# A decode step bound by its K and V stream: w1 loaded second, the MLP moved into the first group, weights in contiguous rows

## The chip, the cores and the metric

The kernel runs on one core of a Trainium2 chip; the other cores are idle. A core has five engines with a queue of instructions each: TensorE (PE in the profile, its weight loads PEld), VectorE (DVE), ScalarE (ACT), GpSimd (POOL) and SyncE (SP). They run independently and wait for each other on semaphores. SP and ACT also issue DMAs, which 16 DMA engines carry out; each engine works through the packets of a queue in the order of their issue. The metric is the device time of one execution, in microseconds (us).

## The reference

The layer is the gated sum of an attention over a cache and of an MLP, for a batch of 8 sequences with one new token each. D is 576, there are 32 heads of 128, 4096 cached positions, and the MLP is 4608 wide. All arrays are bf16.

```python
x = A_x                                             # (8, 1, 576)
g = sigmoid((x * gate_w).sum(-1, keepdims=True))
q = (x @ wq) -> (8, 32 heads, 1, 128)               # wq: 576 x 4096
s = q . k_cache * 128 ** -0.5                       # k_cache: 8 x 32 x 4096 x 128
a = (softmax(s) . v_cache) -> (8, 1, 4096) @ wo     # wo: 4096 x 576
y = layernorm(x)
b = gelu(y @ w1 + b1) @ w2 + b2                     # w1: 576 x 4608, w2: 4608 x 576
return g * a + (1 - g) * b
```

The two caches are 268 MB each, the four weights together about 20 MB. Every byte is read once.

## The kernel before

**Groups.** The 256 pairs of a sequence and a head are worked off in NG = 32 groups of HB = 8 heads of one sequence. A group needs 8 MB of K and 8 MB of V. The 128 partitions hold 8 heads times 16 stretches of 256 positions, so each partition reads one contiguous run of the cache. K comes in two halves of 4 MB, each into a buffer of its own (`KB`, two of them), V in one load of 8 MB into the single buffer `VB`. A fourth large buffer, `RB`, holds one weight after the other: wq, w1, w2, wo.

**Scores.** VectorE multiplies K by the broadcast query in 8 chunks of 32 positions per partition (`mult`, line 448) into the tile `p1`. TensorE sums the products with an identity as its weights: one weight load and 8 matmuls to a chunk (`p_sum`, lines 459 and 461; the helper `held` puts seven of them on line 179). VectorE adds up the last 16 columns (`reduce`, 466). A product chunk has to wait until the sums two chunks earlier have read its half of `p1`.

**Softmax, PV, gathering.** VectorE and ScalarE make the softmax (483 to 499). TensorE multiplies the probabilities by V in 64 matmuls with a weight load each (`pv`, 509); ScalarE evicts (521); TensorE gathers the heads' rows (527), VectorE normalizes one group later (`norm`, 532).

**Order on the engines.** There is no scheduler. Each call of `op` appends an instruction to one engine's list, and each engine runs its list in that order, waiting where an operand is not ready. `aside` does the same with a second semaphore. The function `between(c)` is called between chunks and slips other work into the lists at that place. SP's list holds nearly all loads, so that a load whose buffer is not free holds back all loads behind it. A K half waits for the last product of the half before in its buffer (`k_done`), a V load for the PV of the group before (`v_done`).

**The weights' schedule.** SP issues x, then wq, K and V of group 0. x is transposed on TensorE (`transposed`, 368) so that the contraction runs over partitions: partition p of slice kt stands for row 128 kt + p of the weight. The Q projection takes 40 matmuls (405). Its end frees `RB` for w1 (411). q is broadcast to the partitions by `q_of(b)` for each of the 8 sequences, two matmuls (426) and an eviction (430); the first runs ahead of group 0, the others between its chunks. The up projection (`up_proj`, 547), 216 pairs of a weight load and a matmul of 8 columns, is spread over groups 1 and 2 (`UP`, `NUP`). Behind it w2 takes `RB`. The GELU (`act_h`, 551) and the down projection (`down_proj`, 144 matmuls on line 571) lie in group 3 (`DN`), and wo follows.

**Loops.** The instructions of TensorE are written out for groups 0 to 3, and groups 4 to 29 are turns of a loop (`LOOP`, `emit_loop`). VectorE's loop covers groups 1 to 29. `emit_loop` turns each wait that grows by the same step from turn to turn into a wait on a computed value. The last two groups are written out, and their V comes in smaller parts.

Of the kernel before, what the change touches and what calls it, by code (L numbers as in the profile page):

```python
# [12 lines left out]
B = 8  # L13
# [28 lines left out]
class Stream:  # L42
# [98 lines left out]
def bass_gated_mix__mha_block_cached__mixer_channel_mlp__decode_kernel(  # L141
# [45 lines left out]
    RB = sb("RB", [128, 9 * F // 2], BF16)  # L187
    wq_sb = view(RB, 0, [128, 4, SK])
    wq_t = view(RB, 4 * SK, [128, SK // 2])
    w1_sb = view(RB, 0, [128, 4, F])  # L190
    w1_t = view(RB, 4 * F, [128, F // 2])
    w2_sb = view(RB, 0, [128, NJ, D])
    wo_sb = view(RB, 0, [128, H, D])
    p1 = sb("p1", [128, 2, CT, DH], BF16)
# [66 lines left out]
    def load(engine, dst, src, name, waits=()):  # L261
        return op(engine, lambda e: e.dma_start(dst, src), waits, dma=(nc.alloc_semaphore(name), 16))  # L262
# [7 lines left out]

    c_b2 = op("gpsimd", lambda e: e.memset(b2_4[:], 0.0))
    c_g4 = op("gpsimd", lambda e: e.memset(g4[:], 0.0))
    ld_x = load("sync", x_sb, x_flat, "ld_x")
    ld_gw = load("scalar", gw8, bcast(gate_w), "ld_gw")
    ld_b1 = load("scalar", b1_sb[:, :], B_b1.rearrange("(p j) -> p j", j=NJ), "ld_b1")
    def halves(w):

        return w[512:576, :].rearrange("r (s n) -> (r s) n", s=2)

    ld_wq = [load("sync", wq_sb, A_wq[0:512, :].rearrange("(kt p) n -> p kt n", p=128), "ld_wqa"),  # L280
             load("sync", wq_t, halves(A_wq), "ld_wqb")]


    def kv_src(cache, n):
# [12 lines left out]
    def load_v(n):  # L297
        nV[0] += 1
        src = kv_src(A_v_cache, n)
        t = op("sync", lambda e: e.dma_start(VB[:, :, :], src), [v_done.get(n - 1)], dma=(sV, 16 * nV[0]))  # L300
        v_land[n] = [(t, VB, 0, 0, NTT)]

    def load_v_part(n, buf, at, t0, t1, waits):
# [8 lines left out]

    load_k(0)
    load_k(1)
    load_v(0)


    def memset(engine, ap, value):
        return op(engine, lambda e: e.memset(ap, value))
# [48 lines left out]
    def transposed(src, srcz, col, waits):  # L368
        last = None
        for kt in range(NKF + 2):  # L370
            o = up_ps[:, col + kt * B:col + (kt + 1) * B]
            i = src[:, kt * 128:(kt + 1) * 128] if kt < NKF else srcz[:, kt - NKF, :, :].rearrange("b r s -> b (r s)")
            last = aside("tensor", lambda e, o=o, i=i: e.matmul(o, lhsT=i, rhs=ident[0:B, 0:B], start=True, stop=True),
                      waits if kt == 0 else ())
        return last
# [22 lines left out]
    for half in range(2):  # L398
        for h in range(4):
            for kt in range(NKT):  # L400
# [7 lines left out]
        a_Q.append(aside("scalar", lambda e, half=half: e.activation(  # L408
            out=Q4[:, half * 512:(half + 1) * 512], in_=tr_ps[half][:, :], func=ACT.Copy, scale=inv_sqrt_dh), [p_Q]))

    ld_w1 = [load("sync", w1_sb, B_w1[0:512, :].rearrange("(kt p) f -> p kt f", p=128), "ld_w1a", [p_Q]),
             load("sync", w1_t, halves(B_w1), "ld_w1b")]


    last = NG - 1
    UP, NUP = 1, 2
    DN = UP + NUP
    AP = 30
    LOOP = {"tensor": DN + 1, "vector": 1}
    SLOT = {"tensor": 16, "vector": 128}  # L420

    a_qb, v_mult, v_red, p_sum, v_nm, a_exp, v_P, p_pv, a_ev, p_oz, v_norm, v_rs, p_z, v_rz = ({} for _ in range(14))
# [1 line left out]
    def q_of(b):  # L424
        for i in range(2):
            t = aside("tensor", lambda e, i=i: e.matmul(
                qb_ps[64 * i:64 * i + 64, :], lhsT=Sel[:, b, :],
                rhs=bass.AP(tensor=Q4, offset=i * DH, ap=[[pstride(Q4), 128], [2 * DH, NHG], [1, DH]]),
                start=True, stop=True), [*a_Q, c_Sel, a_qb.get(b - 1)] if i == 0 else ())
        a_qb[b] = aside("scalar", lambda e: e.activation(out=q_bc[:, b, :], in_=qb_ps[:, :], func=ACT.Copy), [t])  # L430
# [109 lines left out]
    def up_proj(j0, j1):  # L540
        for jt in range(j0, j1):
            for kt in range(NKF + 2):
                o, n, at = up_ps[:, jt * B:(jt + 1) * B], 128, kt * F + jt
                if kt >= NKF:
                    o, n, at = up_ps[64 * (kt - NKF):64 * (kt - NKF) + 64, jt * B:(jt + 1) * B], 64, NKF * F + jt
                w = bass.AP(tensor=RB, offset=at, ap=[[pstride(RB), 128], [NJ, n]])
                st["p_up"] = aside("tensor", lambda e, w=w, o=o, kt=kt: e.matmul(  # L547
                    o, lhsT=w, rhs=yT_sb[:, kt, :], start=(kt == 0), stop=(kt >= NKF)),
                    [*ld_w1, v_yT] if jt == kt == 0 else ())
# [13 lines left out]
            out=hT_sb[:].rearrange("p f b -> p (f b)"), in0=hb, in1=t2, op=ALU.mult), [t])  # L563

    def load_w2():
        st["ld_w2"] = load("sync", w2_sb, B_w2.rearrange("(p j) n -> p j n", j=NJ), "ld_w2", [st["p_up"]])

    def quarters(lhsT, w, first, stop, waits):

# [52 lines left out]


    done_a = [0]
    q_of(0)
    q_group(0)
    for n in range(NG):
        for e, l0 in LOOP.items():
            if l0 <= n <= AP:
                S.marks.setdefault(e, []).append(len(S.ops[e]))  # L630

        def between(c, n=n):
            if c == 1 and 1 <= n < last:
                norm(n - 1)
            if n == last and c == NCK:
                load_v_part(n, KB[0], 0, 0, NTK, [k_done[NKH * n]])
                t0 = NTK
                for nt in V_LAST:
                    load_v_part(n, VB, t0 - NTK, t0, t0 + nt, [p_pv[n - 1]])
                    t0 += nt  # L640
            if UP <= n < UP + NUP:
                i = (n - UP) * NC + c
                up_proj(i * NJ // (NUP * NC), (i + 1) * NJ // (NUP * NC))
            if n == DN and c == 1:
                act_h()
            if n == DN and c >= NC - 3:
                down_proj((c - NC + 3) * NJ // 3, (c - NC + 4) * NJ // 3)
            if n >= AP and c % NCK == 2 and done_a[0] < NHG - 1:
                a_proj(done_a[0])
                done_a[0] += 1  # L650
            if n == 0 and c + 1 < B:
                q_of(c + 1)

        scores(n, between)
        if n < last:
            q_group(n + 1)
        softmax(n)
        if n < last:
            total(n)
        if n < last - 1:  # L660
            load_k(NKH * (n + 1))
            load_k(NKH * (n + 1) + 1)
            pv(n, (0,))
            evict(n)
            gather(n)
            if n == UP + NUP - 1:
                load_w2()
            if n + 1 < last - 1:
                load_v(n + 1)
        if n == last - 2:  # L670
            load_v_part(last - 1, VB, 0, 0, NTK, [v_done[n]])
        if n == last - 1:
            load_k(NKH * last)
            load_k(NKH * last + 1)
            load_v_part(n, VB, NTK, NTK, NTT, [v_done[n - 1]])
            pv(n, (0,))
        if n == DN:
            b_out()
            load_wo()
        if n == last - 4:  # L680
            load_b2()
            b_gate()
# [64 lines left out]
```

## Time and profile before

| | |
|---|---|
| median of 3 runs | 1302.79 us (1302.63 to 1303.39) |
| profiled execution | 1302.9 us, of which the span from first to last instruction is 1301.0 |
| mean granted clock of TensorE | 0.844 |
| busy: TensorE matmul, VectorE, ScalarE, GpSimd | 812.0, 849.9, 71.1, 9.6 us |
| DMA | 557.18 MB, mean 428 GB/s |
| K half, from issue to landing (median of 64) | 26.6 us |
| V load, from issue to landing (median of 30) | 31.6 us |

A line such as `24.78 4.49 DVE L448 TENSOR_TENSOR ... x2` reads: start, length, engine and line, operation, tiles written and read, how many instructions were merged. An engine's name with a q behind it is its sequencer, which waits or issues. In windows of time the columns are the window, its length, the busy time of TensorE, its weight loads, VectorE, ScalarE and GpSimd with the instructions in brackets, the granted clock of TensorE, the DMA engines' share of busy time and GB/s. A DMA queue's line gives packets, MB and the packets' time as a share of 16 engines; q1 is SP's, q10 ACT's, q8 fetches instructions.

### The profile page before, as it was taken

The numbers are of one execution on the slowest core, as the hardware profiler recorded it, in microseconds if no ns is written. First come the engines' busy times: TensorE is split into PE (matmuls) and PEld (weight loads), VectorE is DVE, ScalarE is ACT, GpSimd is POOL, SyncE is SP. The second block draws the span as 40 slices with busy tenths as digits, with TensorE's granted clock in tenths as the row PEclk, the third lists the DMA queues.
The fourth block names the chain that finished last, engine by engine and source line by source line (L and its number), as shares of the span: only waits on it lengthen the run. The fifth ranks groups of instructions, "written<-read, shape, count | busy, mean of one in ns | idle before, by whom it ended". The sixth has DMA issues, their size and how long they took to land.

```text
span 1301.0 us, 10743 instructions
## 1 busy us (share of the span) xinstructions
PE 812.0 (62%) x5020; PEld 169.5 (13%) x3228; DVE 849.9 (65%) x1073; ACT 71.1 (5%) x160; POOL 9.6 (1%) x19
## 2 busy tenths in 40 slices
PE   3658746366656565756665765666666666576566
PEld 0113201100111110111110111110011110011112
DVE  3657566277666668666668766667766667766684
ACT  3100000000000000000000000000000000000000
POOL 0000010000000000000000000000000000000000
PEclk8868887688887898888889888789878888978898
DMA  9999999999999999999999999999999999999997
GB/s 398 420 454 422 427 428 443 410 433 432 435 437 429 428 433 432 441 429 433 426 433 434 433 439 427 428 434 434 433 434 433 433 427 433 431 440 429 428 432 321
DMA packets 20894, 557.18 MB, mean 428 GB/s; under 512 B 2048, under 2 KB 6160, under 8 KB 7056
## 3 DMA queue, kind: packets, MB, share of 16 engines
q1 hardware_dynamic: 20624, 556.95, 99.6%
q8 instruction: 10, 0.16, 0.1%
q10 hardware_dynamic: 256, 0.03, 0.0%
q14 instruction: 4, 0.03, 0.0%
HBM read 556.96 MB, written 0.01 MB: 428 GB/s over the span
## 4 chain that ended last, share of the span: by engine, by line
DMA 69%; DVE 18%; PE 9%; issue 3%; SPq 0%; DVEq 0%; ACT 0%
DMA KB<-in_A_k_cache_dram 67%; DVE p L448 16%; PE psb L179 7%; DVE s_sb L466 2%; DMA VB<-in_A_v_cache_dram 2%; PE psb L459 1%; SPq L262 0%; DVEq L134 0%; PE psb L509 0%; DVE P L495 0%; PE psb L571 0%; PE psb L547 0%; PE psb L516 0%; ACT E L492 0%; DVE mA L483 0%
## 5 line engine op out<-in xcount | busy, mean ns | idle before, releaser
L448 DVE TENSOR_TENSOR p<-KB,q_n 128x4096 bf16<-128x4096 bf16 x256 | 582.0, 2284 | 318.1 <-DMA KB<-in_A_k_cache_dram 309.0
L179 PE MATMUL psb<-p,ident 128*128 128x512 bf16 x1792 | 484.4, 416 | 0.0
L459 PE MATMUL psb<-p,ident 128*128 128x512 bf16 x256 | 110.2, 431 | 283.2 <-DVE p L448 283.0
L466 DVE TENSOR_REDUCE s_sb<-psb 128x32 f32<-128x512 f32 x256 | 175.1, 684 | 84.7 <-PE psb L179 84.7
L509 PE MATMUL psb<-VB,P 128*32 128x512 bf16 x1984 | 178.8, 539 | 8.5 <-DMA VB<-in_A_v_cache_dram 8.5
L459 PEld LDWEIGHTS psb<-p,ident 128*128 128x128 bf16 x256 | 26.1, 102 | 699.1 <-DVE p L448 620.0
L516 PE MATMUL psb<-rs,ones 128*128 128x8 f32 x64 | 18.7, 365 | 151.3 <-DVE rs L499 151.3
L509 PEld LDWEIGHTS psb<-VB,P 128*32 128x32 bf16 x1984 | 65.2, 131 | 108.9 <-issue 86.5
L495 DVE TENSOR_SCALAR P<-E,own 128x256 bf16<-128x256 bf16 x248 | 51.6, 283 | 17.9 <-ACT E L492 17.9
L527 PE MATMUL psb<-selO,O_sb 128*128 128x8 f32 x256 | 34.4, 261 | 22.6 <-ACT O_sb L521 22.6
L516 PEld LDWEIGHTS psb<-rs,ones 128*128 128x128 f32 x64 | 15.7, 304 | 203.1 <-DVE rs L499 202.2
L436 ACT ACTIVATE q_n<-q_bc 128x128 bf16<-128x128 bf16 x32 | 9.9, 309 | 529.8 <-DVE p L448 529.7
L527 PEld LDWEIGHTS psb<-selO,O_sb 128*128 128x128 f32 x256 | 31.5, 194 | 37.9 <-ACT O_sb L521 37.9
L521 ACT ACTIVATE O_sb<-psb 128x512 f32<-128x512 f32 x32 | 19.1, 596 | 276.1 <-PE psb L509 276.1
L492 ACT ACTIVATE E<-s_sb,mD 128x256 bf16<-128x256 f32 x32 | 16.2, 507 | 145.4 <-DVE mD L491 145.4
L547 PEld LDWEIGHTS psb<-yT_sb,RB 128*128 128x128 bf16 (+1 forms) x216 | 19.8, 165 | 28.3 <-issue 26.3
L441 ACT ACTIVATE OT_sb<-O_n 128x8 bf16<-128x8 bf16 x31 | 7.4, 237 | 233.2 <-DVE O_n L533 233.2
L547 PE MATMUL psb<-yT_sb,RB 128*128 128x8 bf16 (+1 forms) x216 | 19.9, 226 | 0.0
L483 DVE TENSOR_REDUCE mA<-s_sb 128x1 f32<-128x256 f32 x32 | 13.4, 420 | 1.1
L498 DVE TENSOR_REDUCE es<-E 128x1 f32<-128x256 bf16 x32 | 13.1, 411 | 0.0
L499 DVE TENSOR_SCALAR rs<-own,es 128x8 f32<-128x8 f32 x32 | 7.5, 234 | 1.1
L592 POOL TENSOR_TENSOR Q<-Q,b 104x144 f32<-104x144 f32 x1 | 0.6, 589 | 1009.6 <-DMA b<-in_B_b_dram 1009.6
(76 smaller groups left out, 106.4 us busy)
## 6 DMA issues: line engine op xcount, KB each, us to landing
KB<-in_A_k_cache_dram SPq DMA_DIRECT2D x64, 4096.0 KB, 26.6
VB<-in_A_v_cache_dram SPq DMA_DIRECT2D x2, 4096.0 KB, 24.8
RB<-in_B_w_dram SPq DMA_DIRECT2D x1, 5184.0 KB, 34.8
RB<-in_B_w_dram SPq DMA_DIRECT2D x1, 4608.0 KB, 45.9
RB<-in_A_wo_dram SPq DMA_DIRECT2D x1, 4608.0 KB, 44.5
RB<-in_A_wq_dram SPq DMA_DIRECT2D x1, 4096.0 KB, 12.6
KB<-in_A_v_cache_dram SPq DMA_DIRECT2D x1, 4096.0 KB, 18.9
VB<-in_A_v_cache_dram SPq DMA_DIRECT2D x2, 1024.0 KB, 22.0
```

Source lines behind the costliest of these rows:

```text
L179: return e.add_instruction(mybir.InstMatmult(name=nc.get_next_instruction_name(), engine=mybir.EngineType.PE, ins=[e.lower_ap(rhs), e.lowe ...
L448: v_mult[n, c] = op("vector", lambda e: e.tensor_tensor(out=p1[:, par, :, :], in0=KB[u % NKH][:, t0:t0 + CT, :], in1=qb, op=ALU.mult), [k_ ...
L459: fn = lambda e, r=r: e.matmul(tr_ps[par][:, :], lhsT=ident[:, :], rhs=r, start=True, stop=False)
L466: v_red[n, c] = op("vector", lambda e: e.tensor_reduce(out=s_sb[:, c * CT:(c + 1) * CT], in_=tr_ps[par][:, :].rearrange("p (t c) -> p t c" ...
L483: t = op("vector", lambda e: e.tensor_reduce(out=mA[:, 0:1], in_=s_sb[:, :], axis=AX.X, op=ALU.max), [v_red[n, NC - 1], c_mA])
L492: a_exp[n] = op("scalar", lambda e: e.activation(out=E[:, :], in_=s_sb[:, :], func=ACT.Exp, bias=mD[:, 0:1], scale=1.0), [v_nm[n], v_P.get ...
L495: v_P[n] = op("vector", lambda e, h=h: e.tensor_scalar(out=(P if n < NG - 1 else P_last)[:, :, h, :], in0=E[:, :].rearrange("p (q t) -> p ...
L509: p_pv[n] = op("tensor", lambda e, o=o, tq=tq, at=at, buf=buf: e.matmul(o, lhsT=(P if n < last else P_last)[:, tq, :, :].rearrange("p h t ...
L516: p_z[n] = op("tensor", lambda e: e.matmul(oz_ps[:, HB:2 * HB], lhsT=ones[:, :], rhs=rs[:, :], start=True, stop=True), [v_rs[n], v_norm.ge ...
L521: a_ev[n] = op("scalar", lambda e: e.activation(out=O_sb[:].rearrange("p t d -> p (t d)"), in_=o_ps[n // last][:, :], func=ACT.Copy), [p_p ...
L527: p_oz[n] = op("tensor", lambda e, tt=tt: e.matmul(o, lhsT=O_sb[:, tt, :], rhs=selO[:, tt, :], start=(tt == 0 and n < last), stop=(tt == T ...
L547: st["p_up"] = aside("tensor", lambda e, w=w, o=o, kt=kt: e.matmul(o, lhsT=w, rhs=yT_sb[:, kt, :], start=(kt == 0), stop=(kt >= NKF)), [*l ...
```

## The change

- The layout of wq and w1 in SBUF: partition p now holds rows 4p to 4p + 3 of the first 512 rows, one contiguous run of 32 or 36 KB, where before it held rows p, 128 + p, 256 + p and 384 + p in runs of 8 or 9 KB. x and y are transposed to match: slice kt takes every fourth column.
- w1 goes into `VB`, and SP loads it right behind wq, with no wait. The load of x moves from SP to ACT, ahead of gate_w and b1.
- SP's order at the start becomes wq, w1, K of group 0, then w2 into `RB` (waiting for the Q projection), then V of group 0 (waiting for the up projection, which reads w1 out of `VB`).
- All eight `q_of` and the whole up projection stand ahead of group 0 on TensorE, followed by `act_h`.
- The down projection lies in group 0, a quarter after each of the chunks 3 to 6; wo is loaded after group 0, ahead of V of group 1.
- TensorE's loop begins at group 1.

```diff
-    w1_sb = view(RB, 0, [128, 4, F])
-    w1_t = view(RB, 4 * F, [128, F // 2])
+    w1_sb = view(VB, 0, [128, 4, F])
+    w1_t = view(VB, 4 * F, [128, F // 2])
...
-    ld_x = load("sync", x_sb, x_flat, "ld_x")
+    ld_x = load("scalar", x_sb, x_flat, "ld_x")
...
-    ld_wq = [load("sync", wq_sb, A_wq[0:512, :].rearrange("(kt p) n -> p kt n", p=128), "ld_wqa"),
+    ld_wq = [load("sync", wq_sb, A_wq[0:512, :].rearrange("(p kt) n -> p kt n", kt=4), "ld_wqa"),
              load("sync", wq_t, halves(A_wq), "ld_wqb")]
+    ld_w1 = [load("sync", w1_sb, B_w1[0:512, :].rearrange("(p kt) f -> p kt f", kt=4), "ld_w1a"),
+             load("sync", w1_t, halves(B_w1), "ld_w1b")]
...
-        t = op("sync", lambda e: e.dma_start(VB[:, :, :], src), [v_done.get(n - 1)], dma=(sV, 16 * nV[0]))
+        t = op("sync", lambda e: e.dma_start(VB[:, :, :], src), [v_done.get(n - 1) if n else st["p_up"]], dma=(sV, 16 * nV[0]))
...
     load_k(0)
     load_k(1)
-    load_v(0)
...
-            i = src[:, kt * 128:(kt + 1) * 128] if kt < NKF else srcz[...]
+            i = src[:, kt:NKF * 128:NKF] if kt < NKF else srcz[...]
...
-    ld_w1 = [load("sync", w1_sb, B_w1[0:512, :].rearrange("(kt p) f -> p kt f", p=128), "ld_w1a", [p_Q]),
-             load("sync", w1_t, halves(B_w1), "ld_w1b")]
...
-    UP, NUP = 1, 2
-    DN = UP + NUP
-    LOOP = {"tensor": DN + 1, "vector": 1}
+    LOOP = {"tensor": 1, "vector": 1}
...
-                w = bass.AP(tensor=RB, offset=at, ap=[[pstride(RB), 128], [NJ, n]])
+                w = bass.AP(tensor=VB, offset=at, ap=[[pstride(VB), 128], [NJ, n]])
...
-        st["ld_w2"] = load("sync", w2_sb, B_w2.rearrange("(p j) n -> p j n", j=NJ), "ld_w2", [st["p_up"]])
+        st["ld_w2"] = load("sync", w2_sb, B_w2.rearrange("(p j) n -> p j n", j=NJ), "ld_w2", [p_Q])
...
-    q_of(0)
-    q_group(0)
+    for b in range(B):
+        q_of(b)
+        if b == 0:
+            q_group(0)
+        up_proj(b * NJ // B, (b + 1) * NJ // B)
+    act_h()
+    load_w2()
+    load_v(0)
...
-            if UP <= n < UP + NUP:
-                i = (n - UP) * NC + c
-                up_proj(i * NJ // (NUP * NC), (i + 1) * NJ // (NUP * NC))
-            if n == DN and c == 1:
-                act_h()
-            if n == DN and c >= NC - 3:
-                down_proj((c - NC + 3) * NJ // 3, (c - NC + 4) * NJ // 3)
+            if n == 0 and 3 <= c <= 6:
+                down_proj((c - 3) * NJ // 4, (c - 2) * NJ // 4)
...
-            if n == 0 and c + 1 < B:
-                q_of(c + 1)
...
-            if n == UP + NUP - 1:
-                load_w2()
+            if n == 0:
+                b_out()
+                load_wo()
...
-        if n == DN:
-            b_out()
-            load_wo()
```

More of the change, by code (lines that the diff above doesn't have):

```diff
@@ L371, in transposed @@
             o = up_ps[:, col + kt * B:col + (kt + 1) * B]
-            i = src[:, kt * 128:(kt + 1) * 128] if kt < NKF else srcz[:, kt - NKF, :, :].rearrange("b r s -> b (r s)")
+            i = src[:, kt:NKF * 128:NKF] if kt < NKF else srcz[:, kt - NKF, :, :].rearrange("b r s -> b (r s)")
             last = aside("tensor", lambda e, o=o, i=i: e.matmul(o, lhsT=i, rhs=ident[0:B, 0:B], start=True, stop=True),
```

## The prediction

> **What bounds the kernel now.** I read the page first: engine shares, slices, traffic, chain.
>
> ```profile
> span 1301.0 us, 10743 instructions
> ...
> PE 812.0 (62%) x5020; PEld 169.5 (13%) x3228; DVE 849.9 (65%) x1073; ACT 71.1 (5%) x160; POOL 9.6 (1%) x19
> ...
> DMA  9999999999999999999999999999999999999997
> GB/s 398 420 454 422 427 428 443 410 433 432 435 437 429 428 433 432 441 429 433 426 433 434 433 439 427 428 434 434 433 434 433 433 427 433 431 440 429 428 432 321
> DMA packets 20894, 557.18 MB, mean 428 GB/s; under 512 B 2048, under 2 KB 6160, under 8 KB 7056
> ...
> DMA 69%; DVE 18%; PE 9%; issue 3%; SPq 0%; DVEq 0%; ACT 0%
> ```
>
> No engine is busy over 65%, while the DMA line is full from the first slice to the last but one. The chain names VectorE for 18%, but those steps only wait for the next transfer. Then the busy time by stage, to see whether any stage has a hole that a better order could fill. Columns: window, its length, busy time of five engines, clock, DMA share, GB/s.
>
> ```profile
> 67.00:100.00 33.00, 19.86 (x120) 7.20 (x78) 19.05 (x15) 0.24 (x1) 0.00 (x0) 0.67 1.04 448
> 100.00:133.00 33.00, 28.55 (x232) 13.42 (x183) 23.89 (x32) 1.65 (x4) 0.00 (x0) 0.90 0.97 420
> 133.00:166.00 33.00, 24.35 (x170) 8.22 (x126) 19.36 (x29) 3.65 (x7) 4.48 (x4) 0.79 1.01 435
> 166.00:199.00 33.00, 15.38 (x212) 4.11 (x179) 17.66 (x26) 2.10 (x3) 2.25 (x1) 0.82 0.98 423
> 265.00:1265.00 1000.00, 630.49 (x3614) 112.88 (x2157) 687.26 (x858) 42.09 (x102) 1.24 (x2) 0.85 1.00 432
> ```
>
> A share swings a little above and below 1.00 because whole packets are booked to a window. There is no hole: the groups 1 to 3, where the up and down projections lie now, have the share of the 1000 us behind them. So the time is the first packet's start, plus 557 MB at the engines' rate, plus a tail behind the last packet. The change moves the same 557 MB. It can win only at the start and in the rate of wq, w1 and instruction packets; it can lose by opening a hole.
>
> **The start.** What SP issues, and the first 12 us:
>
> ```profile
> 0.74 0.38 SPq L262 DMA_DIRECT2D p<-in_A_x_dram  x1
> 1.18 0.96 SPq L262 DMA_DIRECT2D RB<-in_A_wq_dram  x2
> 2.18 1.10 SPq L295 DMA_DIRECT2D KB<-in_A_k_cache_dram  x2
> ...
> 20.57 0.93 SPq L262 DMA_DIRECT2D RB<-in_B_w_dram  x2
> ...
> 0.00:2.00 2.00, 0.00 (x0) 0.00 (x0) 0.31 (x2) 0.24 (x1) 1.23 (x10) 1.00 0.03 9
> 2.00:4.00 2.00, 0.00 (x0) 0.00 (x0) 1.86 (x7) 1.99 (x3) 0.36 (x3) 1.00 0.89 230
> 4.00:6.00 2.00, 0.00 (x0) 0.00 (x0) 0.97 (x5) 1.98 (x4) 0.00 (x0) 1.00 1.00 409
> 6.00:8.00 2.00, 0.00 (x0) 0.00 (x0) 0.00 (x0) 1.97 (x3) 0.00 (x0) 1.00 1.03 435
> 8.00:10.00 2.00, 0.30 (x6) 0.24 (x6) 0.74 (x4) 0.70 (x5) 0.00 (x0) 1.00 0.99 418
> 10.00:12.00 2.00, 0.32 (x6) 0.24 (x6) 0.21 (x1) 1.09 (x6) 0.00 (x0) 1.00 1.03 430
> ```
>
> *x goes to ACT's queue.* wq is then SP's first issue, at 0.74 instead of 1.18: 0.44 us sooner for the whole stream. It gains at least 0.3 (x's small packets still share the engines), at most 0.5. I take 0.4. On ACT, x stands ahead of gate_w and b1, which go out about 0.4 us later; gate_w feeds ACT's sigmoid, ahead of x's transposition, and those results are wanted only when wq has landed, 3.6 us after they are ready (the wait of L405 below). b1 is wanted at about 51. Both cost nothing; without that cover, 0.4.
>
> *wq in contiguous rows.* Its 8 KB rows become one 32 KB run per partition, which is what a K load has. From 4 to 12 us wq ran at (409 + 435 + 418 + 430)/4 = 423 GB/s against 432: 4.19 MB take 9.91 against 9.71 us, 0.2 us. The 2 to 4 window carries 0.46 MB where 0.86 would fit, 0.9 us lost, of which 0.2 is the idle share. If long runs mend the remaining 0.7, the gain is 0.9. Bounds 0 and 0.9, taken 0.4: the steady rows show 0.2 for certain, the ramp may be latency as well as short rows.
>
> *w1 in contiguous rows.* Rows of 9 KB become 36 KB. The nearest rows are wq's: at the same 2%, 4.72 MB gain 0.2 us; bounds 0 and 0.4. Taken 0.2. The stationary operands of x and y are now read with a step of 4, in 12 transpositions of 0.05 us each: nothing, behind the same 3.6 us of cover.
>
> **TensorE's loop.** Groups 1 to 3 leave the written-out code. Instruction packets, by two windows (40 to 210 us, then 205 to 1220):
>
> ```profile
> q1 hardware_dynamic: 2429, 72.91, 99.8%
> q8 instruction: 7, 0.11, 0.3%
> ```
>
> ```profile
> q1 hardware_dynamic: 15264, 438.64, 100.3%
> q10 hardware_dynamic: 64, 0.01, 0.0%
> ```
>
> Seven packets of 16 KB came in while TensorE ran written-out code, none while it looped. A packet held one engine 0.3% x 16 x 170 us / 7 = 1.2 us. By the code a group is some 220 weight loads and matmuls: 8 chunks of 9, 64 pairs for PV, about 20 for the sums and the gathering. Four groups, with 432 for the up projection, 288 for the down projection and some 90 before, make 1690, or 240 to a packet. Three groups less save 2.7 packets: spread evenly, 0.2 us; all on the engine that ends last, 3.2; on other engines than the last, 0. I take 0.2, since three packets of seven need not meet on one of 16 engines.
>
> The Trainium skill, Runtime: NRT & Kernel Launch, Instruction fetch mechanics, speaks against this part: a taken branch out of the two-page window forces a fetch, so written-out code is to be preferred. By it 29 loop-backs instead of 26 would fetch again what is saved, and the sum would be 1.0 rather than 1.2 us. The second window, 26 turns without one q8 packet, disagrees, and the measurement decides.
>
> **The moved work: does it open a hole?** After the change the queue holds wq, w1, K of group 0 (two halves), w2, V of group 0, K of group 1, wo, V of group 1. At 432 GB/s: wq 10.9 us, w1 12.3, a K half 9.7, w2 12.3, V 19.4. From 1.8 (2.2, where the 0.89 share puts the first full packet, less 0.4), with 0.3 for the ramp: wq ends at 13.0, w1 25.3, K 44.7, w2 57.0, V 76.4, K of group 1 at 86.1 and 95.8. Each load must be issued about 1.0 us (1.18 to 2.2) before its turn. The price of TensorE's work, with two windows for its granted clock:
>
> ```profile
> 15.16 5.38 PE L405 MATMUL psb<-RB,p 128*8 128x512 bf16 x40 [3.64 <-DMA RB<-in_A_wq_dram]
> ...
> 27.13 0.61 PE L459 MATMUL psb<-p,ident 128*128 128x512 bf16 x1 [5.49 <-DVE p L448]
> 30.57 0.41 PE L426 MATMUL psb<-Q,Sel 128*64 128x512 bf16 x2
> ...
> 36.39 11.53 SPq L295 DMA_DIRECT2D KB<-in_A_k_cache_dram  x2
> 54.23 0.23 DVE L499 TENSOR_SCALAR rs<-own,es 128x8 f32<-128x8 f32 x1
> 55.33 6.49 PE L509 MATMUL psb<-VB,P 128*32 128x512 bf16 x64 [0.22 <-DMA VB<-in_A_v_cache_dram]
> ...
> 82.00:84.00 2.00, 2.00 (x11) 0.62 (x6) 0.71 (x4) 0.24 (x1) 0.00 (x0) 0.50 0.99 426
> 83.53 1.04 PEld L547 LDWEIGHTS psb<-yT_sb,RB 128*128 128x128 bf16 x11 [0.26 <-issue]
> 92.00:94.00 2.00, 2.00 (x14) 0.55 (x6) 2.00 (x2) 0.00 (x0) 0.00 (x0) 1.00 1.18 500
> 93.36 1.78 PEld L547 LDWEIGHTS psb<-yT_sb,RB 128*128 128x128 bf16 x18 [1.43 <-issue]
> 160.30 0.39 ACT L554 ACTIVATE Q<-psb 128x288 f32<-128x288 f32 x1
> 166.06 2.25 POOL L562 TENSOR_TENSOR hT_sb<-Q 128x288 bf16<-128x288 f32 x1 [0.55 <-ACT Q L561]
> ...
> 177.15 0.93 PE L571 MATMUL psb<-RB,hT_sb 128*8 128x144 bf16 x48 [1.94 <-DMA RB<-in_B_w_dram]
> ```
>
> - *w2 waits for the Q projection.* wq lands at about 14.3 (15.16 less 0.4 and 0.4), the projection ends 5.4 later, 19.7; w2's turn is at 44.7. Nothing behind it on SP is due before.
> - *V of group 0 waits for the up projection.* w1 lands 12.0 after wq, about 26.3. 216 pairs of weight load and matmul at 1.78/18 = 0.099 us are 21.4, seven q broadcasts at 0.41 are 2.9: end at 50.6. V must be issued by 56.0. Spare 5.4 us, the smallest of all; with no cover it costs one for one.
> - *K of group 1 waits for group 0's products.* Group 0's sums now start at 50.6 instead of 27.1, 23.5 later. Its K buffers come free at 36.4 + 23.5 = 59.9 and (SP's second issue of that row) 47.6 + 23.5 = 71.1, due at 75.4 and 85.1.
> - *The down projection in group 0.* h is ready 8.0 us (160.30 to 168.31) after the up projection, 58.6; w2 lands at 58. Its first quarter stands behind the fourth chunk, 60 to 62, and so does not wait. Four times 36 matmuls at 0.93/48 are 2.8 us beside VectorE, in place of the q broadcasts. wo can go out at about 71; its turn is 95.8.
> - *V of group 1 waits for PV of group 0.* The softmax ends at 54.5 + 23.5 = 78.0, V lands at 77.4, PV takes 6.5: 84.5. With some 12 for wo it is due at 107. That issue may be held on SP while wo's short rows drain, as a K issue is now: the row below holds two issues from 218.28 to 241.77, with wo in flight, and the window that has it shows no hole beyond wo's slower rows. Costs 0.
>
> ```profile
> 218.28 23.49 SPq L295 DMA_DIRECT2D KB<-in_A_k_cache_dram  x2
> 232.00:265.00 33.00, 12.79 (x90) 3.87 (x76) 10.28 (x22) 1.34 (x3) 0.00 (x0) 0.64 1.04 420
> ```
>
> From group 1 on everything stands as now against the DMA stream, so its shift reaches the last output unchanged.
>
> **Sum.** 0.4 + 0.4 + 0.2 + 0.2 = 1.2 us sooner. The profiled execution took 1302.9 (span 1301.0 and 1.9 around it), 0.1 over the median 1302.79. So 1301.6 by the median; bounds of this case 0.5 and 2.2 us, 1300.6 to 1302.3.
>
> **Rivals.**
> - *Slower: the up projection ends late and V of group 0 opens a hole.* It decides from 5.4 us on: to lose 0.2% it must end 1.2 + 2.6 + 5.4 = 9.2 us late. If the 216 pairs cost twice as much in one run (0.2 us), the end moves by 21.4 to 72 and the hole is 16 us: 1318. For it: 460 instructions in a row, more than the trace ever shows at this pace, and the clock falling after the idle wait for w1. Against it: PV issues 128 in 6.5 us, and the 11 loads at 83.53, at a granted clock of 0.50, cost 0.095 us each, the 18 at 93.36, at a clock of 1.00, 0.099. The Trainium skill, TensorE: Matmul & The Clock Gate, Part 1: after an idle window of about 3.4 us the array runs at half rate until it has been busy as long. By that rule a pair would double while cold; these rows show no such effect on these small matmuls. Chance 0.11, typically 1306 or more.
> - *Faster by over 0.2%.* The ramp mends fully (0.9) and two saved instruction packets were on the engine that ends last (2.4 instead of 0.2): 0.4 + 0.9 + 0.4 + 2.4 = 4.1, about 1299. For it: every such packet delays one engine for good in a stream without holes. Against: nothing shows them on one engine. Chance 0.13.
> - *The layouts do nothing.* The rate of wq and w1 stays, the first packet starts where it did because of x's packets: 1302.6. The 6 to 8 window, 435 GB/s with 8 KB rows, speaks for it. Chance 0.14.
>
> **How the numbers follow.** The likeliest case has 0.62, own range 1300.6 to 1302.3. A measurement of this kernel can tell about 0.2%, 2.6 us, from no change: within it lie the likeliest case and the idle layouts, 0.76; faster 0.13; slower 0.11. The range, 1299.8 to 1303.3, leaves out most of the slow case and half of the fast one.
>
> **What would show it.** wq's first issue at about 0.74 and the 2 to 4 window well above 230 GB/s; the Q projection's first matmul at 14.3 rather than 15.16; the last L547 at about 50 and SP's first V issue right behind it, with DMA shares near 1.00 from 50 to 110; five or fewer q8 packets before the loop; a span of about 1299.8 instead of 1301.0. A DMA share under 0.9 between 56 and 60 would prove me wrong, and so would TensorE waits called issue inside the up projection.

## The result and the profile after

| | before | after |
|---|---|---|
| median | 1302.80 us (22 runs, 1302.55 to 1303.93) | 1300.97 us (22 runs, 1300.67 to 1302.29) |
| ratio | | 0.9986, 95% interval 0.9979 to 0.9992 |
| span of the profiled execution | 1301.0 us | 1299.1 us |
| DMA packets | 20894 | 20124 |
| instruction packets (q8) ahead of the loop | 7 | 5 |

The change gains 1.83 us, 0.14%, and the interval of the ratio leaves out 1. That is 0.6 us more than the 1.2 forecast, and less than the 0.2% (2.6 us) up to which the prediction counted a time as no change. The page of the changed kernel has the same form as before: no engine above 65%, and a DMA line that is full up to the last slice.

```profile
span 1299.1 us, 10783 instructions
...
PE 813.6 (63%) x5020; PEld 166.9 (13%) x3228; DVE 849.8 (65%) x1073; ACT 68.7 (5%) x158; POOL 6.1 (0%) x19
...
DMA  9999999999999999999999999999999999999997
GB/s 405 434 418 422 447 426 438 418 435 435 438 438 428 425 435 434 442 428 430 430 433 433 438 430 440 421 434 429 440 438 426 435 424 435 436 434 438 419 434 335
DMA packets 20124, 557.14 MB, mean 429 GB/s; under 512 B 2048, under 2 KB 6160, under 8 KB 7056
```

What SP issues up to group 1, in the changed kernel (start, length, queue, line, what is written and read):

```profile
0.74 0.88 SPq L262 DMA_DIRECT2D RB<-in_A_wq_dram  x2
1.67 1.18 SPq L262 DMA_DIRECT2D VB<-in_B_w_dram  x2
...
20.09 0.33 SPq L262 DMA_DIRECT2D RB<-in_B_w_dram  x1
50.12 0.33 SPq L302 DMA_DIRECT2D VB<-in_A_v_cache_dram  x1
59.76 11.53 SPq L297 DMA_DIRECT2D KB<-in_A_k_cache_dram  x2
71.33 0.43 SPq L262 DMA_DIRECT2D RB<-in_A_wo_dram  x1
85.68 19.51 SPq L302 DMA_DIRECT2D VB<-in_A_v_cache_dram  x1
```

The moved work on TensorE and the end of group 0's softmax on VectorE. (Line numbers have shifted: 542 is the up projection, 566 the down projection, 494 the softmax's end, 504 PV, 605 the last V parts.)

```profile
14.81 5.25 PE L405 MATMUL psb<-RB,p 128*8 128x512 bf16 x40 [2.43 <-DMA RB<-in_A_wq_dram]
...
27.12 2.22 PE L542 MATMUL psb<-yT_sb,VB 128*128 128x8 bf16 x24 [5.97 <-issue]
...
47.86 2.23 PE L542 MATMUL psb<-yT_sb,VB 128*128 128x8 bf16 x24
61.62 0.74 PE L566 MATMUL psb<-RB,hT_sb 128*8 128x144 bf16 x36
...
79.66 5.97 PE L504 MATMUL psb<-VB,P 128*32 128x512 bf16 x64 [1.18 <-DMA VB<-in_A_v_cache_dram]
```

```profile
77.60 0.23 DVE L494 TENSOR_SCALAR rs<-own,es 128x8 f32<-128x8 f32 x1
```

Windows of the changed kernel; the last two columns are the DMA share and GB/s, and the one before them the granted clock:

```profile
0.00:2.00 2.00, 0.00 (x0) 0.00 (x0) 0.31 (x2) 0.00 (x0) 1.23 (x10) 1.00 0.71 184
2.00:4.00 2.00, 0.00 (x0) 0.00 (x0) 1.72 (x6) 1.91 (x3) 0.36 (x3) 1.00 0.88 328
4.00:6.00 2.00, 0.00 (x0) 0.00 (x0) 0.45 (x4) 1.98 (x4) 0.00 (x0) 1.00 0.65 279
...
56.00:60.00 4.00, 2.11 (x9) 0.19 (x2) 4.00 (x4) 0.00 (x0) 0.00 (x0) 1.00 1.04 449
...
100.00:133.00 33.00, 12.68 (x67) 1.94 (x35) 16.89 (x26) 0.82 (x2) 0.00 (x0) 0.78 1.05 432
265.00:1265.00 1000.00, 630.27 (x3612) 112.23 (x2156) 685.82 (x857) 42.09 (x102) 1.15 (x2) 0.85 1.00 432
```

From 56 to 60, where a late V of group 0 would show, the share is 1.04: no hole. The steady stretch runs at 432 GB/s, as before. So the gain lies at the two ends of the stream, and the end is where most of it is. Four 1-us windows of the last stretch, the six microseconds from 1290 in one window, and the matmuls that wait for the last part of V. First the kernel before:

```profile
1290.00:1296.00 6.00, 4.60 (x82) 3.42 (x82) 0.21 (x1) 0.60 (x1) 0.00 (x0) 0.78 0.63 246
...
1293.00:1294.00 1.00, 1.00 (x14) 1.00 (x11) 0.00 (x0) 0.00 (x0) 0.00 (x0) 0.68 0.62 242
1294.00:1295.00 1.00, 1.00 (x19) 0.94 (x19) 0.00 (x0) 0.00 (x0) 0.00 (x0) 0.50 0.15 57
1295.00:1296.00 1.00, 0.84 (x26) 0.73 (x24) 0.00 (x0) 0.00 (x0) 0.00 (x0) 0.50 0.09 35
```

```profile
1296.41 0.38 PE L610 MATMUL psb<-p,VB 128*128 128x8 bf16 x8 [0.26 <-DMA VB<-in_A_v_cache_dram]
```

Then the changed kernel:

```profile
1290.00:1296.00 6.00, 5.05 (x120) 3.96 (x112) 0.35 (x2) 0.60 (x1) 0.00 (x0) 0.73 0.48 186
...
1292.00:1293.00 1.00, 1.00 (x22) 0.96 (x21) 0.00 (x0) 0.00 (x0) 0.00 (x0) 0.87 0.69 266
1293.00:1294.00 1.00, 0.81 (x24) 0.68 (x23) 0.00 (x0) 0.00 (x0) 0.00 (x0) 0.50 0.21 80
1294.00:1295.00 1.00, 0.58 (x16) 0.41 (x13) 0.12 (x1) 0.00 (x0) 0.00 (x0) 0.50 0.00 0
```

```profile
1294.46 0.38 PE L605 MATMUL psb<-p,VB 128*128 128x8 bf16 x8 [0.26 <-DMA VB<-in_A_v_cache_dram]
```

One engine of 16 that works for a whole microsecond makes a share of 0.06. Before, after most engines had ended by 1294, two or three worked on in the next microsecond (0.15) and one or two in the one after it (0.09). After, the share falls from 0.69 to nothing in two microseconds. The last matmuls start 1.95 us sooner (1296.41 to 1294.46), but the time that an average engine still worked behind 1290 fell by only 0.90 us (6 x 0.63 = 3.78 to 6 x 0.48 = 2.88). The other 1.05 is no shorter stream: it is that the engines end together.

### The profile page after: what moved, and what is told of

Read it like the earlier page. It is cut to its first block, busy times and chain, and to the rows that moved or that the text cites. A ratio compares the mean times of both kernels' runs of the same rounds, so it can differ in the third digit from the quotient of the medians.

```text
span 1299.1 us, 10783 instructions
## 1 busy us (share of the span) xinstructions
PE 813.6 (63%) x5020; PEld 166.9 (13%) x3228; DVE 849.8 (65%) x1073; ACT 68.7 (5%) x158; POOL 6.1 (0%) x19
## 2 busy tenths in 40 slices
DMA packets 20124, 557.14 MB, mean 429 GB/s; under 512 B 2048, under 2 KB 6160, under 8 KB 7056
## 4 chain that ended last, share of the span: by engine, by line
DMA 67%; DVE 18%; PE 11%; issue 3%; SPq 0%; DVEq 0%; ACT 0%
DMA KB<-in_A_k_cache_dram 63%; DVE p L443 15%; PE psb L179 7%; DVE s_sb L461 2%; DMA VB<-in_B_w_dram 2%; DMA VB<-in_A_v_cache_dram 2%; PE psb L542 2%; PE psb L454 1%; DVEq L134 0%; SPq L262 0%; PE psb L504 0%; PE psb L421 0%; SPq L302 0%; DVE P L490 0%; PE psb L566 0%
## 5 line engine op out<-in xcount | busy, mean ns | idle before, releaser
L542 PE MATMUL psb<-yT_sb,VB 128*128 128x8 bf16 (+1 forms) x216 | 20.1, 230 | 6.0 <-issue 6.0
L542 PEld LDWEIGHTS psb<-yT_sb,VB 128*128 128x128 bf16 (+1 forms) x216 | 18.4, 166 | 10.4 <-issue 9.3
```

## The experiments

Two theories were set against each other. A, the prediction's: the end follows the mean load of the 16 DMA engines, so a packet of instructions costs a sixteenth of its 1.1 us. B: the engine that lags most sets the end, so such a packet costs nothing or about 1.1 us. "Before" is between 1302.81 and 1302.90 in the comparisons below. The times of one kernel scatter by about 1 us or more, mostly outside the span from first to last instruction; the spans scatter by 0.3 to 1.0 us. So a difference of 0.2 or 0.3 us between medians is hardly clear of the scatter.

**The parts, undone one at a time.** In the changed kernel, x goes back to SP's queue:

```diff
-    ld_x = load("scalar", x_sb, x_flat, "ld_x")
+    ld_x = load("sync", x_sb, x_flat, "ld_x")
```

> The changed kernel with x loaded on SP again, ahead of wq. Theory A (the transfers' total sets the time, and each part counts with its own share): wq is issued 0.4 us later, so 0.4 us slower than the changed kernel, about 1301.4. Theory B (the one DMA engine that lags most sets the end): the same 0.4, changed by up to 0.5 either way if x's eight packets fall on other engines. Rival, the start is bound by the first packets' latency and not by the issue: 1301.0.

Measured 1301.15 us (ratio 0.9988, 0.9979 to 0.9997): 0.18 more than the changed kernel, within the spread of either. Then wq and w1 in their old rows, with the transposition to match:

```diff
-    ld_wq = [load("sync", wq_sb, A_wq[0:512, :].rearrange("(p kt) n -> p kt n", kt=4), "ld_wqa"),
+    ld_wq = [load("sync", wq_sb, A_wq[0:512, :].rearrange("(kt p) n -> p kt n", p=128), "ld_wqa"),
...
-    ld_w1 = [load("sync", w1_sb, B_w1[0:512, :].rearrange("(p kt) f -> p kt f", kt=4), "ld_w1a"),
+    ld_w1 = [load("sync", w1_sb, B_w1[0:512, :].rearrange("(kt p) f -> p kt f", p=128), "ld_w1a"),
...
-            i = src[:, kt:NKF * 128:NKF] if kt < NKF else srcz[:, kt - NKF, :, :].rearrange("b r s -> b (r s)")
+            i = src[:, kt * 128:(kt + 1) * 128] if kt < NKF else srcz[:, kt - NKF, :, :].rearrange("b r s -> b (r s)")
```

> The changed kernel with wq and w1 in the old layout, rows of 8 and 9 KB, and x and y transposed to match. Theory A: w1's packets held the 16 engines 11.29 us in the old layout against 10.93 in the new one, wq's steady rows differ by 0.2: 0.55 us slower than the changed kernel, about 1301.5. If the ramp of the first packets were mended by long rows, 1.2 slower. Rival, the layouts do nothing: 1301.0. The first matmul of the Q projection should start 0.1 to 0.3 us later than 14.81.

Measured 1301.28 us (0.9988, 0.9979 to 0.9997): 0.31 more, hardly clear of the scatter either. Then TensorE's loop over groups 4 to 29, as before the change:

```diff
-    LOOP = {"tensor": 1, "vector": 1}
+    LOOP = {"tensor": 4, "vector": 1}
```

> The changed kernel with TensorE's groups 1 to 3 written out again, the loop from group 4. Two or three more instruction packets of 16 KB. Theory A: each counts a sixteenth of its 1.1 us, 0.2 us slower, about 1301.2. Theory B: each delays one engine by 1.1 us for good, and the end moves with the engine that lags most: anywhere from 0 to 1.5 us slower, as they fall.

Measured 1302.35 us (0.9995, 0.9986 to 1.0004): 1.38 more. The part to which the prediction gave 0.2 of 1.2 us carries most of the gain.

**The parts, done alone.** The kernel before, with x on ACT's queue and with the rows of wq and w1 and the transposition of the change, and nothing else:

```diff
-    ld_x = load("sync", x_sb, x_flat, "ld_x")
+    ld_x = load("scalar", x_sb, x_flat, "ld_x")
...
-    ld_wq = [load("sync", wq_sb, A_wq[0:512, :].rearrange("(kt p) n -> p kt n", p=128), "ld_wqa"),
+    ld_wq = [load("sync", wq_sb, A_wq[0:512, :].rearrange("(p kt) n -> p kt n", kt=4), "ld_wqa"),
...
```

> The kernel before with x on ACT and wq and w1 in contiguous rows alone; order, buffers and loop as before. Theory A: 0.4 + 0.55 us faster than before, about 1301.85. Theory B: the same for the mean of the engines, while the slowest one may keep its lag or lose it: 1301.2 to 1302.5. If the new order itself brings something, this falls short of the changed kernel by more than the 0.2 of the instruction packets.

Measured 1301.90 us (0.9993, 0.9984 to 1.0002): 0.9 to 1.0 sooner than before. Compared with the changed kernel with its loop at group 4 (1302.35), which differs from it in the order alone, the new order brings nothing (it is 0.45 slower). The order and the loop without x and rows, which is the changed kernel with the first two edits of this section together:

```diff
-    ld_x = load("scalar", x_sb, x_flat, "ld_x")
+    ld_x = load("sync", x_sb, x_flat, "ld_x")
...
-    ld_wq = [load("sync", wq_sb, A_wq[0:512, :].rearrange("(p kt) n -> p kt n", kt=4), "ld_wqa"),
+    ld_wq = [load("sync", wq_sb, A_wq[0:512, :].rearrange("(kt p) n -> p kt n", p=128), "ld_wqa"),
...
```

> The changed kernel with x back on SP's queue and wq and w1 back in rows of 8 and 9 KB: what is left of the change is the order of the loads and TensorE's loop over groups 1 to 29. Undone one by one, x cost 0.18 and the rows 0.31 us. If these add up, 1301.5 beside 1302.8 for the kernel before: the loop and the order then carry 1.3 of the 1.8 us. The prediction's sum gives 0.2 to them, so 1302.6. Theory B allows 1301.0 to 1302.4, by where the instruction packets fall.

Measured 1301.40 us (0.9989, 0.9980 to 0.9998), as expected from adding (1301.5), and not the 1302.6 of the prediction's sum.

**Is it one lagging engine?** An extra load on ACT's queue at the start, into a free stretch of `p1`, with the first products waiting for it. On 17 partitions it should run on one engine. (The Trainium skill, DMA: Bandwidth & Descriptors, section Why a DMA increments its semaphore by 16 and not by 1, under How many engines (k): the largest count up to 16 that divides the partitions, here 1.) The control puts the same bytes on 16 partitions, with `p1[64:80, 1, 0:17, :]` and t=17.

```diff
+    ld_more = load("scalar", p1[64:81, 1, 0:16, :], A_k_cache[0, 0, 0:272, :].rearrange("(p t) d -> p t d", t=16), "ld_more")
...
-            + ([v_yT, p_yT, p_Q] if n == 0 and c < 2 else []))
+            + ([v_yT, p_yT, p_Q, ld_more] if n == 0 and c < 2 else []))
```

> The changed kernel with one more load at the start on ACT's queue: 17 partitions of 4 KB of K into an unused part of the tile p1, 70 KB in all, which group 0's first products wait for. Seventeen partitions cannot be split over several engines, so one engine carries all of it, 17 x 0.16 = 2.7 us. Theory A (total of the transfers): 2.7/16 = 0.2 us slower, 1301.1. Theory B (the engine that lags most): the engine is late by 2.7 us to the end; less what it was ahead of the slowest, which the tail shows as up to 2.1 us: 0.6 to 2.7 us slower, 1301.6 to 1303.7.

> The control of the run before: the same 70 KB, at the same place, from 16 partitions of 4.25 KB, one packet for each of the 16 engines. Both theories: 0.17 us on every engine, 0.2 us slower, 1301.1.

Measured 1302.47 us on one engine and 1301.60 spread: the same 70 KB cost 0.87 us more where one engine carries them. The control itself costs 0.6, where a sixteenth of 2.6 us was expected; it lies in the mean of the engines (3.48 against 2.88 in the table below) and stays unexplained. Windows of the two, one engine first, then the control:

```profile
1290.00:1296.00 6.00, 4.29 (x80) 3.63 (x80) 0.00 (x0) 0.60 (x1) 0.00 (x0) 0.71 0.57 223
...
1294.00:1295.00 1.00, 1.00 (x34) 1.00 (x33) 0.00 (x0) 0.00 (x0) 0.00 (x0) 0.50 0.09 33
```

```profile
1290.00:1296.00 6.00, 4.11 (x102) 3.44 (x98) 0.19 (x1) 0.60 (x1) 0.00 (x0) 0.70 0.58 226
...
1294.00:1295.00 1.00, 0.73 (x21) 0.56 (x18) 0.00 (x0) 0.00 (x0) 0.00 (x0) 0.50 0.03 10
```

The six-microsecond shares agree (0.57 and 0.58), so the mean load is the same; what differs is the tail in the microsecond from 1294, 0.09 against 0.03. The trace agrees that one engine carried the load: at the end of the first K half, about 36 us, one engine of 16 stands 2.7 us behind their mean, and 2.0 us still at 1273 (how this is read is said below the table).

**How many instruction packets?** The loop from group 3 and from group 2 (`"tensor": 3` and `"tensor": 2`):

> The changed kernel with TensorE's loop over groups 3 to 29 instead of 1 to 29, nothing else: two groups more of written-out code, by the 240 instructions to a packet some 1.8 instruction packets more than in the changed kernel (8 there, 11 with the loop from group 4). Theory A (only the mean load of the engines counts): 1.8 packets of 0.07 us each, 1301.1. Theory B (the DMA engine that lags most sets the end): the packets come at other moments, so the time follows the engines that they meet and need not grow evenly with the number of packets: anywhere from 1301.0 to 1302.4, and the 1-us windows of the last stretch show, where it is slow, a DMA share of 0.05 to 0.2 in the last microsecond or two instead of a fall to 0 within one.

> The changed kernel with TensorE's loop over groups 2 to 29 instead of 1 to 29, nothing else: one group more of written-out code, about 0.9 instruction packets. Theory A: 1301.05. Theory B: between 1301.0 (the packet meets an engine that does not lag) and about 1302.1 (it meets the one that lags most, 1.1 us), and the tail of the DMA share says which.

Measured 1302.28 (0.9996, 0.9987 to 1.0005) and 1302.23 us (the same ratio and interval). One group more of written-out code costs 1.26 us, the second 0.05, the third 0.07. A mean load would climb in even steps; this is one step, and then level. The step is clear of the scatter: the spans of all runs are 1298.6 to 1299.1 us for the changed kernel and 1299.8 to 1300.5 with the loop from group 2. The queue of instruction packets between 20 and 230 us in the changed kernel and with the loop from group 2, and the latter's tail:

```profile
q8 instruction: 5, 0.08, 0.2%
```

```profile
q8 instruction: 6, 0.10, 0.2%
```

```profile
1290.00:1296.00 6.00, 3.90 (x72) 3.65 (x72) 0.17 (x1) 0.26 (x1) 0.00 (x0) 0.57 0.49 190
...
1292.00:1293.00 1.00, 1.00 (x14) 1.00 (x10) 0.00 (x0) 0.00 (x0) 0.00 (x0) 0.50 0.65 252
1293.00:1294.00 1.00, 1.00 (x14) 1.00 (x14) 0.00 (x0) 0.00 (x0) 0.00 (x0) 0.50 0.22 86
1294.00:1295.00 1.00, 0.99 (x38) 0.90 (x34) 0.00 (x0) 0.00 (x0) 0.00 (x0) 0.50 0.06 23
```

The windows from 1292 to 1294 are those of the changed kernel within 0.04 (0.65 and 0.22 against 0.69 and 0.21). Then there is a share of 0.06 where the changed kernel has 0.00: one engine of 16, for one microsecond.

**The packet or the loop?** The last question was whether it is the sixth packet that costs, or the place where the loop begins. The first quarter of the down projection five times, with the loop left as it is:

```diff
-                down_proj((c - 3) * NJ // 4, (c - 2) * NJ // 4)
+                for i in range(5 if c == 3 else 1):
+                    down_proj((c - 3) * NJ // 4, (c - 2) * NJ // 4, c == 3 and i < 4)
```

The third argument closes the accumulation, so that the next one starts afresh.

> The changed kernel, with the first quarter of the down projection (36 weight loads and 36 matmuls behind the fourth chunk of group 0) done five times instead of once, each time from a fresh start; the result is the same. TensorE's loop still covers groups 1 to 29, no load is added or moved. It adds 288 instructions of TensorE ahead of the loop, more than the 240 to an instruction packet, so six instruction packets before the loop instead of five, or seven. The 4 x 0.74 = 3.0 us of work delay the sums of group 0; K of group 1 was issued at 59.8 and 71.3 and is due at 75 and 85, V of group 1 at 85.7 and due at 105, so no hole is opened, and a DMA share near 1.00 from 67 to 133 us shows that. Theory A (mean load of the engines): one packet of 1.1 us over 16 engines, 1301.04. Theory B (the DMA engine that lags most sets the end; so far every kernel with five such packets ended between 1301.0 and 1301.6, and every one with six or seven between 1301.9 and 1302.8): 1302.2, with a share of about 0.06 left in the 1-us window at 1294, one engine of 16. If instead it was where the loop begins, and not the packet, that cost the 1.3 us, this kernel stays at 1301.0.

Measured 1302.16 us (0.9996, 0.9987 to 1.0005), against 1302.2 by B and 1301.04 by A. Its tail, its packets and the stretch in which a hole would lie:

```profile
67.00:133.00 66.00, 37.87 (x311) 8.30 (x230) 36.89 (x54) 3.94 (x8) 0.00 (x0) 0.78 1.02 423
1290.00:1296.00 6.00, 3.78 (x72) 3.62 (x72) 0.00 (x0) 0.39 (x1) 0.00 (x0) 0.63 0.49 189
...
1294.00:1295.00 1.00, 1.00 (x34) 1.00 (x33) 0.00 (x0) 0.00 (x0) 0.00 (x0) 0.50 0.06 25
```

```profile
q8 instruction: 6, 0.10, 0.2%
```

All kernels without a hole side by side. "Mean" is six times the share from 1290 to 1296, the time that an average engine still works behind 1290; "lag" is the start of the last matmuls, less 1290, less the mean.

| kernel | packets, 20 to 230 us | median us | last matmuls | mean | lag |
|---|---|---|---|---|---|
| after | 5 | 1300.97 | 1294.46 | 2.88 | 1.58 |
| x_on_sync | 5 | 1301.15 | 1294.58 | 3.18 | 1.40 |
| old_rows | 5 | 1301.28 | 1294.66 | 3.42 | 1.24 |
| up_54_more (below) | 5 | 1301.29 | 1294.09 | 2.94 | 1.15 |
| order_and_loop | 5 | 1301.40 | 1294.67 | 3.48 | 1.19 |
| all_engines | 5 | 1301.60 | 1294.77 | 3.48 | 1.29 |
| down_first_five | 6 | 1302.16 | 1295.74 | 2.94 | 2.80 |
| loop_from_2 | 6 | 1302.23 | 1295.41 | 2.94 | 2.47 |
| loop_from_3 | 7 | 1302.28 | 1295.49 | 3.12 | 2.37 |
| loop_from_4 | 7 | 1302.35 | 1295.73 | 3.00 | 2.73 |
| before_x_rows | 7 | 1301.90 | 1295.43 | 3.06 | 2.37 |
| before | 7 | 1302.80 | 1296.41 | 3.78 | 2.63 |
| one_engine | 5, and 70 KB | 1302.47 | 1295.77 | 3.42 | 2.35 |

The lag takes two values, 1.15 to 1.6 and 2.35 to 2.8, with nothing between. The step is about the length of one instruction packet (1.02 to 1.10 us for each of the changed kernel's eight before 1300). The sixth packet, or a load on one engine, makes the step; the seventh adds nothing. The mean moves by 0.9 at most.

**Why the sixth?** The packet records of the kept traces answer most of it. They name no engine, but each engine writes one packet of 4 bytes at the end of each load on SP's queue, so that every load leaves 16 end times, one for each engine. Three more instruction packets come behind the loop, in every kernel of the table, at about 1228, 1260 and 1289 us:

```profile
q8 instruction: 1, 0.02, 0.3%
```

That is the window from 1270 to 1292 of the changed kernel. So eight, nine or ten packets come before the stream ends at 1294 to 1296. Each of the first eight makes one more engine late, and the slowest takes no second step. At 1224 us it is 0.7 to 1.4 us behind the mean of the 16, whether five, six or seven packets had come (1.43 in the changed kernel, 0.99 with the loop from group 2, 0.88 from group 3); only in one_engine it is 2.2. The ninth packet falls on an engine that is late already. With seven packets ahead of the loop the ninth is the one at 1260, and the slowest engine goes from 0.6 to 1.0 us behind the mean to 2.1 to 2.4 there (from 0.80 to 2.07 with the loop from group 3). With six the ninth is the one at 1289: in loop_from_2 and down_first_five the packets of the engine that ends last, followed back one by one, lead through it. With five there is no ninth. The tenth falls on a second late engine, which makes two that end late and not one that ends later: the share from 1294 is 0.06 with six packets and 0.11 to 0.15 with seven, here with the loop from group 3:

```profile
1294.00:1295.00 1.00, 1.00 (x38) 0.93 (x35) 0.00 (x0) 0.00 (x0) 0.00 (x0) 0.50 0.12 45
```

It is as if eight engines took the instruction packets in turn; which eight, the traces do not say.

**How far is V of group 0 from a hole?** First 54 of the 216 pairs of the up projection computed twice, then all of them (without the condition on b):

```diff
         up_proj(b * NJ // B, (b + 1) * NJ // B)
+        if b < 2:
+            up_proj(b * NJ // B, (b + 1) * NJ // B)
```

> The changed kernel with the first 54 pairs of the up projection computed twice, the same result. The up projection ends 5.3 us later, at about 55.3, and V of group 0 is issued then; its first packet is due at 57.6, an issue 1.0 earlier. No hole: the same time, 1301.0, but for 108 more instructions on TensorE, which may move one instruction packet (0 to 1 us by theory B). If the spare time were smaller than 5.3, every us over it would show.

> The changed kernel with the whole up projection computed twice, the same result. It ends 21.4 us later, V of group 0 is issued at 71.5 instead of 50.1. The spare time is about 6.5 us (from 50.1 to 56.6), so the DMA queue runs empty for 14.9 us and the kernel takes about 1316; two more instruction packets add 0.1 (theory A) or up to 1 us (theory B). If the group's compute has slack to take the hole up later, less.

Measured 1301.29 us (0.9986, 0.9977 to 0.9995) and 1314.68 us (1.0089, 1.0075 to 1.0102). V's issue and the windows, first 54 pairs, then all:

```profile
54.71 0.33 SPq L302 DMA_DIRECT2D VB<-in_A_v_cache_dram  x1
```

```profile
40.00:60.00 20.00, 20.00 (x162) 12.20 (x148) 4.07 (x4) 3.84 (x7) 3.37 (x5) 0.51 1.00 426
```

```profile
69.45 0.33 SPq L302 DMA_DIRECT2D VB<-in_A_v_cache_dram  x1
```

```profile
40.00:60.00 20.00, 20.00 (x211) 17.18 (x209) 2.41 (x2) 2.39 (x4) 0.00 (x0) 0.50 0.87 374
60.00:70.00 10.00, 10.00 (x103) 8.46 (x101) 0.00 (x0) 1.01 (x2) 0.05 (x1) 0.50 0.01 2
```

With 4.6 us more in front (54.71 against 50.12) there is no hole. With 19.3 more the stream stops at 57.4 (20 x 0.87 from 40), and the time rises by 13.7. So 19.3 - 13.7 = 5.6 us of the delay were covered: the spare time. This kernel fetches two instruction packets more by 110 us (seven, not five), but they do not make the step here: its last matmuls start at 1307.62, the share from 1302 to 1308 is 0.70, and the lag, reckoned from 1302, is 1.42.

## Why the prediction was right, point by point

- *The bound.* Right: 432 GB/s in the steady stretch in both kernels, and no hole from 50 to 133 (a share of 1.02 over these 83 us).
- *x to ACT, 0.4.* wq was issued at 0.74, as said, and the gain was there in part: with x back on SP the mean of the engines ends 0.30 later (3.18 against 2.88), but they end closer together, so that the median loses 0.18, and the Q projection's first matmul 0.11 (14.92 against 14.81). The Q projection moved by 0.35 (15.16 to 14.81), not by 0.8 to 14.3. The first packet starts sooner, but the start does not run at the steady rate: the windows from 0 to 6 have shares of 0.71, 0.88 and 0.65.
- *wq's rows 0.4, w1's rows 0.2.* The start was only partly mended, nearer to the lower bound. The 2 to 4 window rose from 230 to 328 GB/s, but 4 to 6 fell from 409 to 279. By the 4-byte packets the engines end the main part of wq at 12.47 us on average, against 13.02 before: 0.55, where 0.8 was forecast for x and wq together. The old rows alone cost 0.54 in the mean (3.42 against 2.88), where 0.6 was forecast for wq and w1. The terms do not add up, though: done alone, x and rows lower the mean by 3.78 - 3.06 = 0.72 us, and undone together they raise it by 3.48 - 2.88 = 0.60, against 1.0 forecast for the three.
- *TensorE's loop: "2.7 fewer instruction packets ... I take 0.2".* This is the mis-sized term. The packets fell from seven to five, as said; the loop's part is worth 1.26 to 1.38 us (loops from groups 2 to 4) because one DMA engine, and not the mean of 16, sets the end. The prediction had "0.2 if spread evenly, up to 3.2 if all on the engine that ends last", and chose the even end because "three packets of seven need not meet on one of 16 engines". The packets ahead of the loop indeed did not meet; but the prediction counted these alone, and the three behind the loop meet engines that are late already as soon as more than five have come before. The kernel's own tail, shares of 0.15 and 0.09 behind 1294, showed such engines before the change, and the prediction did not read it.
- *The faster rival* named that mechanism with two packets' worth; one packet's worth came. That the forecast of 1.2 and the 1.83 measured are near each other is in part luck, two errors that partly cancel: about 0.3 too much for the start (a mean gain of 0.90 against 1.2), and 1.05 too little for the lag.
- *The Trainium skill*, Runtime: NRT & Kernel Launch, Instruction fetch mechanics, calls the crossing of a 16 KiB block of instructions mostly hidden and would have code written out rather than looped. It is hidden from TensorE here, which was at work for 23.00 of the 23.12 us from 27.00 to 50.12, in which two such packets came. But the sixth packet still costs 1.26 us where the DMA stream is the bound: three runs with one to three groups more written out and one with 288 more instructions disagree with it. Its 256 instructions to a block agree with 288 more instructions making one packet more.
- *V of group 0.* Right. The up projection ended at 50.1 (50.6 forecast), V was issued at 50.12, and the spare time of 5.4 us came out at 5.6, by what the whole up projection costs when it is doubled. The slower rival's price, "72, hole 16 us, 1318", came out at 69.45 and 1314.7, by a pair that is a little cheaper than 0.099 us: in the window below of line 542 alone, 20.13 us for 216 pairs, 0.093 each, at a granted clock of 0.50.

```profile
23.00:54.00 31.00, 20.13 (x216) 18.38 (x216) 0.50 1.02 435
```

- *The clock.* The Trainium skill's rule (TensorE: Matmul & The Clock Gate, Part 1) agrees in its first half: TensorE stood idle for 5.97 us ahead of the up projection, and its granted clock then was 0.50. In the second half it does not: the clock stayed at 0.50 for the 31 us of the row above, with TensorE at work for 26.9 of them. And these pairs did not take twice as long, as the prediction's two rows had said; in them the clock is not the bound.
- *K of group 1, the down projection, V of group 1.* K issued at 59.76 and by 71.3 (59.9 and 71.1 forecast), the first quarter at 61.62 without a wait for a transfer, wo at 71.33 (71), the softmax's end at 77.60 (78.0). PV then waited 1.18 us for V, which landed some 2 us later than the 77.4 of the forecast, and V of group 1 was issued at 85.68 (84.5). That issue held SP until 105.19, with wo in flight, and cost nothing: the share from 100 to 133 is 1.05.
- *The layouts do nothing.* Wrong as a whole (0.9 us in before_x_rows), near the truth for x alone.

What stays open: the 0.6 us of the spread extra load; why the ninth instruction packet meets an engine that has had one; and why x and the rows lower the median by 0.9 in the old kernel and by 0.43 in the new one (there the lag grows as the mean falls, 1.19 to 1.58). Part of the 1.58 belongs to the one profiled execution: its slowest engine was 0.50 us behind the mean at the end of wq already, in up_54_more, whose start is the same, only 0.13, and its span of 1299.1 is the longest of the 22, whose median is 1298.8. No version among the runs beats the changed kernel.

## What to carry to other kernels

Where a stream over all DMA engines is the bound, read the last few microseconds in 1-us windows: a share that ends in a tail of 0.06 to 0.15 says that one or two engines lag, and a microsecond can be had there with nearly the same bytes. Whatever lands on a single engine, an instruction packet or a load over 17 partitions, is not to be costed at a sixteenth of its length: it costs up to its full length where it meets an engine that is late already, and next to nothing elsewhere (1.26 us for the sixth packet, 0.05 for the seventh). Count such packets to the end of the stream, those behind a loop too. Written-out instructions are traffic as well: a loop that starts sooner can be worth more than better rows.

## What was not expected of the hardware

- An instruction packet of 16 KB holds one DMA engine for 1.02 to 1.10 us, and a stream without holes hardly makes that up: the slowest engine of the changed kernel stood 1.49 us behind the mean at 97 us and 1.43 at 1224. The first eight packets fell on different engines and the ninth on one that was late already, so that one packet more ahead of the loop cost 1.2 us (1302.16 and 1302.23 against 1300.97).
- The first three windows of 2 us ran at 184, 328 and 279 GB/s with rows of 32 KB, against 9, 230 and 409 with rows of 8 KB and x ahead; with rows of 32 KB and x ahead (x_on_sync) it was 9, 279 and 508. What sets this start is not shown.
- 216 pairs of a weight load and a matmul of 8 columns took 0.093 us each at a granted clock of 0.50; 18 such weight loads had taken 0.099 at a clock of 1.00 in the kernel before.
